# Spectral layers of a gated mixing kernel: z copied out of its bank by ScalarE, sum and low part made from the copies, one clamp moved to GpSimd

## The chip, the cores and the metric

The kernel runs on one core of one Trainium2 chip. A core has five engines, each with its own instruction queue that is worked off in order: TensorE (PE in the profile; PEld is its weight loading), VectorE (DVE), ScalarE (ACT), GpSimd (POOL) and SyncE (SP, which here only issues DMAs). The metric is the device time of one execution in microseconds (us). The kernel before takes 2457.5 us, the median of three runs (2455.3 to 2458.45).

## The reference

Two layers share an input and are mixed by a gate. Layer A is the spectral one: a real Fourier transform over 4096 tokens, a two-layer complex perceptron in four blocks of 160 channels on every frequency, a soft threshold, and the inverse transform. Layer B is a gated feed-forward network.

```python
x = A_x                                                  # A_x has shape (2, 1, 4096, 640)
g = _sigmoid((x * gate_w).sum(-1, keepdims=True))
a = _A_ref(x, A_w1, A_b1, A_w2, A_b2)
b = _B_ref(x, B_w_gate, B_w_up, B_w_down)
return g * a + (1 - g) * b

# _A_ref, per frequency; z has real part zr and imaginary part zi
hr = relu(zr @ w1[0] - zi @ w1[1] + b1[0]);  hi = relu(zi @ w1[0] + zr @ w1[1] + b1[1])
or_ = hr @ w2[0] - hi @ w2[1] + b2[0];       oi_ = hi @ w2[0] + hr @ w2[1] + b2[1]
# soft threshold at lam = 0.01, then irfft2
# _B_ref
(_gelu(x @ w_gate) * (x @ w_up)) @ w_down
```

## The kernel before

All matmuls of weight run on numbers that were split in two: a high part, which ScalarE makes by a copy that rounds (`high`, L292), and a low part, source minus high part, which VectorE makes (`low`, L295). A product is then three matmuls: high by high, high by low, low by high.

The program has four parts in time. Up to about 1316 us TensorE does the first two matrices of layer B, with the first stage of the Fourier transform (`a_step`) sprinkled in. From about 1316 to 1760 us come the spectral layers, which the change touches. Then follow the last matrix of layer B together with the second inverse stage, to the end. There is no planner: the order in which the Python code calls the engines is the order of each queue.

**The spectral layers** run as 64 steps, 4 for each of 16 chunks of 256 frequencies; the four steps of a chunk are its four channel blocks, n = 0 to 3. The chunk that is called wide (the second one, steps 4 to 7) has two more columns and a path of its own. One turn i of the loop issues, in this order:

- `main_z` for step i+1. Its core is `fwd2`: the second stage of the Fourier transform for 128 channels of a block, 4 matmuls at L1018 (8 in the trace, which shows each of these twice) into a PSUM bank `pz`, whose first half is the real part of z and whose second half the imaginary part, 256 columns each. Out of the bank come z high (L292), z low (L295), and the sum of both halves: ScalarE copies the second half to `zt` (L1029), VectorE adds the first half (L1030). The sum in turn is split into `zs` high and low, by a closure that `fwd2` returns and that is called later (`sums`). The sum lets three products stand for the four of a complex one.
- `mlp1` for step i: bank `pk` from zs (4 matmuls), copied out by ScalarE to `kc` (L1126); bank `pm` from z (8 matmuls); two adds on VectorE give `hs` (L1133); then `sums()` for step i+1; then relu and split into `h` (ScalarE L1089, VectorE L1090); bank `pl` for the 32 channels per block that do not fit in 128 (5 matmuls), taken out by ScalarE (L1139) and VectorE (L1140).
- `mlp2` for step i-1: two banks `py` of 16 matmuls each, taken out by ScalarE (`m`, L1170) and VectorE (`y`, L1171).
- `rest_of` for step i: relu of the 64 rows that L1140 wrote, to `hB` (L1143) and `hA` (L1144), both on ScalarE, and the low part from them on VectorE (L1145). hA and hB are used by `mlp2` of the next turn.
- In every odd turn, `inv1`: the first inverse stage, four banks `pi` of 3 matmuls each, taken out by ScalarE (L1206) and VectorE (L1208) in turn. In every even turn, `y_split`: y is split into `ys`, two tiles of 640 columns, both high parts on ScalarE, one low part on VectorE and one on GpSimd.
- Once a chunk, in the turn with i = 1 modulo 4 (below the rest turn), `rest`: the same `fwd2`, for the 4 x 32 remaining channels of the next chunk, issued ahead of `main_z`. Its z (named `zz`) and zs go through DRAM (`zld`) and come back four times as `zl` (`zl_load`, two turns ahead of their use). Its closure `end` runs at the end of the turn, ahead of `inv1`, and makes zs with the low part on GpSimd.

There are eight PSUM banks. They are handed out in turn, so a matmul that opens a bank waits for the last reader of what stood there eight hand-outs before. Two engines that read the same bank are ordered one behind the other too. An even turn takes 6 banks (pz, pk, pm, pl, py, py), an odd one 10, the one with `rest` 11. Thus pk takes the bank of the last pl when an odd turn came before it, and waits for the reader L1140; the third pi of an odd turn takes the bank of the same turn's main pz, the fourth that of its pk, and in the rest turn the second that of the rest's pz.

Of the kernel before, what the change touches and what calls it, by code (L numbers as in the profile page):

```python
# [10 lines left out]
F32 = mybir.dt.float32  # L11
F32R = mybir.dt.float32r
AF = mybir.ActivationFunctionType
OP = mybir.AluOpType

P = 128
# [6 lines left out]
CH = 256  # L23
CW = CH + 2
NCH = 8
# [211 lines left out]
def spectral_mix_kernel(ctx: ExitStack, tc: tile.TileContext, a):  # L237
    nc = tc.nc
    out = a["out"]

    def dr(t, off, ap):
        return bass.AP(tensor=t.tensor, offset=t.offset + off, ap=ap)
# [7 lines left out]
    def bank():  # L250
        return psum.tile([P, 512], F32, name="bank", tag="bank")
# [6 lines left out]
    def small(shape, dt=F32, name="small"):  # L258
        return pool.tile(shape, dt, name=name, tag="small", bufs=17)

    def tiny(shape, dt=F32, name="tiny"):
        return pool.tile(shape, dt, name=name, tag="tiny", bufs=15)
# [4 lines left out]
    def st(dst, src):  # L267
        late.append((dst, src))
# [22 lines left out]
    def high(dst, src, scale=1.0):  # L291
        nc.scalar.activation(dst, src, AF.Copy, scale=scale)  # L292

    def low(dst, src, hi, eng=nc.vector):
        eng.tensor_sub(dst, src, hi.bitcast(F32))  # L295

    def split(dst_h, dst_l, src, eng=nc.vector):

        high(dst_h, src)
        low(dst_l, src, dst_h, eng)  # L300

    def by_two(m):
        return m.rearrange("p (k i) -> p i k", k=2)
# [8 lines left out]
    def mms(dst, ops):  # L312
        for i, (l, r) in enumerate(ops):
            nc.tensor.matmul(dst, l, by_two(r), start=i == 0, stop=i == len(ops) - 1)  # L314
# [207 lines left out]
    def x_deep(gr, tp):  # L522


        o = {}
        F = XA[gr, tp] = {}

        def part(k):
# [3 lines left out]
            def tile():  # L532
# [5 lines left out]
                for j, n in enumerate(names):  # L538
                    F[n] = tuple(m[:, h, 320 * j:320 * j + 320] for h in range(2))
                return m  # L540
# [424 lines left out]
    chunks = [(0, 1), (0, 0)] + [(b, c) for b in range(2) for c in range(NCH) if (b, c) > (0, 1)]  # L965

    def zmid(b, c, shape, dt=F32, name="z"):
        return (big if wide(b, c) else mid)(shape, dt, name=name)

    def two(b, c, name):  # L970

        if wide(b, c):
            return [mid([P, 2, CW], F32R, name=name) for h in range(2)]
        t = mid([P, 2, 2, CH], F32R, name=name)
        return [t[:, h] for h in range(2)]
# [3 lines left out]
    def part_of(b, c, k):  # L979

        if not wide(b, c):
            return tiny([P, CH], name=("zt", "kc", "hs")[k])
        if not WT:
            WT.append(mid([P, 3, CW], name="wt"))
        return WT[0][:, k]
# [27 lines left out]
    def fwd2(b, c, o, z, zs=None):  # L1013

        pz = bank()
        for kp in range(4):
            ft = F2[0 if c == 0 and kp == 0 else 1]
            nc.tensor.matmul(pz.rearrange("p (r e k f) -> p k r e f", r=2, e=2, k=4)[:, kp], SC[b, c, kp][:, o:o + P],  # L1018
                             ft.rearrange("p (r e f) -> p r e f", r=2, e=2), start=True, stop=True)
        F = width(b, c)  # L1020
        if F > CH:
            zz = [z[h][:, :, :F].rearrange("p r (e n) -> p r e n", e=2)[..., :P] for h in range(2)]
            pr = pz.rearrange("p (r e n) -> p r e n", r=2, e=2)
        else:
            zz, pr = [z[h][:, :, :F] for h in range(2)], pz.rearrange("p (r n) -> p r n", r=2)
        if zs:
            t = part_of(b, c, 0)
            t4 = t[:, :F].rearrange("p (e n) -> p e n", e=2)[..., :P] if F > CH else t[:, :F]
            nc.scalar.activation(t4, pr[:, 1], AF.Copy)  # L1029
            nc.vector.tensor_add(t4, pr[:, 0], t4)  # L1030
        high(zz[0], pr)
        low(zz[1], pr, zz[0])
        if wide(b, c):
            pn = bank()
            for q in range(2):
                nc.tensor.matmul(pn[:, :4], SC[q, c, 0][:, o:o + P], fny[:, 4 * q:4 * q + 4], start=q == 0, stop=q == 1)
            split(*(z[h][:, :, :F].rearrange("p r (e n) -> p r e n", e=2)[..., P] for h in range(2)),
                  pn[:, :4].rearrange("p (r f) -> p r f", r=2))
            if zs:
                nc.vector.tensor_copy(t[:, :F].rearrange("p (e n) -> p e n", e=2)[..., P], pn[:, :2])  # L1040
        return lambda eng=nc.vector: split(zs[0][:, :F], zs[1][:, :F], t[:, :F], eng)
# [3 lines left out]
    def rest(b, c):  # L1045

        F = width(b, c)
        z = zmid(b, c, [P, 2, 2, F], F32R, name="zz")
        first = (b, c) == chunks[0]
        zs = small([P, 2, F], F32R, name="zs") if first else None  # L1050
        zs = [zs[:, h] if first else tiny([P, F], F32R, name="zs") for h in range(2)]
        sums = fwd2(b, c, 4 * P, [z[:, h] for h in range(2)], zs)
        d = zld[b][c]
        for h in range(2):
            st(dr(d, 3 * CW * h, [[6 * CW, P], [CW, 2], [1, F]]), z[:, h].bitcast(F32))

        def end():
            sums(nc.gpsimd)
            for h in range(2):
                st(dr(d, 3 * CW * h + 2 * CW, [[6 * CW, P], [1, F]]), zs[h].bitcast(F32))  # L1060
        later.append(end)

# [29 lines left out]
    def mlp1(b, c, n, sums):  # L1092
        F = width(b, c)
        z, (sh, sl) = Z.pop((b, c, n))
        w, wl = W1[n], W1L[n]
        t = ZL.pop((b, c, n))

        part = lambda k: (w[:, k:k + P], w[:, LOW1 + k:LOW1 + k + P])

        def group(dst, m):  # L1100
            r = 1 - m
            wh, wlo = part(OUT1[m])
            mms(dst, [(wh, z[0][:, r]), (wh, z[1][:, r]), (wlo, z[0][:, r]), (wl[:98, P + P * m:2 * P + P * m], t[:98, r])])

        def last(dst):

            for r in range(2):
                k = LAST1[r]
                nc.tensor.matmul(dst, w[:, k:k + P], by_two(z[0][:, r, :F]), start=r == 0, stop=False, skip_group_check=True)
                nc.tensor.matmul(dst, w[:, k:k + P], by_two(z[1][:, r, :F]), start=False, stop=False, skip_group_check=True)  # L1110
            nc.tensor.matmul(dst, wl[:, 384:], by_two(t[:, 3]), start=False, stop=True, skip_group_check=True)
        h = two(b, c, "h")
        if wide(b, c):
            if n < 2:
                x = small([P, 2, CW], F32R, name="hl")
                nc.gpsimd.memset(x[64:66, 1].bitcast(F32), 1.0)
                HW[n] = x[:, 0], x[:66, 1]
            hA, hB = HW[n % 2]
        else:
            hA, hB = hl1[n % 2], hl2[n % 2]  # L1120
        H[b, c, n] = (h, hA, hB)
        pk = bank()
        wh, wlo = part(OUT1["k"])
        mms(pk[:, :F], [(wh, sh[:, :F]), (wh, sl[:, :F]), (wlo, sh[:, :F]), (wl[:96, :P], t[:96, 2])])
        kc, hs = part_of(b, c, 1), (small if wide(b, c) else mid)([P, 2, F], name="hs")
        nc.scalar.activation(kc[:, :F], pk[:, :F], AF.Copy)  # L1126
        pm = [bank()] * 2 if F == CH else [bank(), bank()]
        for r in range(2):
            d = pm[r][:, r * CH:(r + 1) * CH] if F == CH else pm[r][:, :F]
            group(d, r)  # L1130
        for r in range(2):
            d = pm[r][:, r * CH:(r + 1) * CH] if F == CH else pm[r][:, :F]
            nc.vector.tensor_add(hs[:, r, :F], d, kc[:, :F])  # L1133
        sums()
        relu_split(h[0], h[1], hs)
        pl = bank()
        last(pl[:, :F])
        hs = part_of(b, c, 2)[:64]
        nc.scalar.activation(hs, pl[64:, :F], AF.Copy)  # L1139
        nc.vector.scalar_tensor_tensor(hs, pl[:64, :F], b1r[:, n:n + 1], hs, op0=OP.add, op1=OP.add)  # L1140

        def rest_of():
            nc.scalar.activation(hB[:64, :F], hs, AF.Relu)  # L1143
            nc.scalar.activation(hA[:64, :F], hs, AF.Relu)  # L1144
            nc.vector.scalar_tensor_tensor(hA[64:, :F], hs, 0.0, hB[:64, :F].bitcast(F32), op0=OP.max,  # L1145
                                           op1=OP.subtract)
        return rest_of
# [443 lines left out]
    for i, (gr, tp) in enumerate(keys):  # L1591
        if deep((gr, tp)) and tp % 2 == FIRST % 2:
            p, f = x_deep(gr, tp)
# [28 lines left out]
    for i, key in enumerate(keys):  # L1622
# [4 lines left out]
        if nxt:  # L1627
            if not i:
                x_raw(nxt)
            z = 7 * (nq - 1)  # L1630
# [13 lines left out]
        for j, t in enumerate(quads):  # L1644
# [10 lines left out]
            n = len(late)  # L1655
# [23 lines left out]
    for ch in range(1, 2 * NCH):  # L1679
        b, c = chunks[ch]  # L1680
# [27 lines left out]
    for i in range(S + 2):  # L1708
# [23 lines left out]
        if 0 <= i - 1 < S:  # L1732
            b, c, n = steps[i - 1]
# [10 lines left out]
    for i in range(len(c_seq)):  # L1744
        n = i + 1 if i + 1 < len(c_seq) else None
# [65 lines left out]
```

## Time and profile before

| | |
|---|---|
| median of 3 runs | 2457.5 us |
| the profiled execution, its own time | 2454.23 us |
| its span, first to last instruction | 2452.4 us |
| PE, PEld, DVE, ACT, POOL busy over the span | 99%, 97%, 81%, 60%, 7% |
| spectral layers | about 1316 to 1760 us |

How to read it: an engine's row gives start and duration of an instruction, and in brackets the idle time of the engine just before it with what ended it. Matmuls are pipelined: a matmul's duration is longer than the distance to the next one, so the distance between starts is what a matmul costs. The profiled execution is 3.3 us shorter than the median of the three runs.

### The profile page before, as it was taken

How to read it: one execution, taken by the hardware profiler on the slowest of the kernel's cores; microseconds unless marked ns; L12 is line 12 of the kernel's file. 1: busy time of each engine (PE TensorE's matmuls, PEld its weight loads, DVE VectorE, ACT ScalarE, POOL GpSimd, SP SyncE). 2: the span in 40 equal slices, each digit the busy share in tenths (PEclk: the TensorE clock that was granted, in tenths of full speed). 3: DMA queues.
4: the chain of work that ended last, by engine and by line, in shares of the span. 5: the costliest groups of instructions: out<-in, count | busy, mean ns of one | idle time of the engine just before them, and what ended most of it. 6: DMA issues, size and time to landing. Idle time of an engine off the chain costs nothing.

```text
span 2452.4 us, 50055 instructions
## 1 busy us (share of the span) xinstructions
PE 2415.7 (99%) x17983; PEld 2388.7 (97%) x17983; DVE 1980.7 (81%) x4175; ACT 1476.4 (60%) x3368; POOL 181.1 (7%) x286
## 2 busy tenths in 40 slices
PE   9999999999999999999999999999999999999999
PEld 9999999999999999999999888988899999999999
DVE  7777778777778888888758778787888988888887
ACT  5544456655556666666546777777755555555554
POOL 0111110000000000000001222212000000000000
PEclk9999999999999999999999999999999999999999
DMA  5665576777777768677765555667964455555443
GB/s 214 244 231 228 220 257 209 261 256 250 260 258 245 255 227 276 233 270 236 254 243 188 172 180 182 186 194 252 312 212 149 151 156 160 168 162 158 150 148 105
DMA packets 341315, 521.78 MB, mean 213 GB/s; under 512 B 28863, under 2 KB 217927, under 8 KB 341067
## 3 DMA queue, kind: packets, MB, share of 16 engines
q1 hardware_dynamic: 321002, 465.30, 57.1%
q0 software_dynamic: 20064, 53.29, 6.0%
q8 instruction: 142, 2.33, 0.4%
q14 instruction: 107, 0.87, 0.1%
HBM read 323.17 MB, written 195.30 MB: 211 GB/s over the span
## 4 chain that ended last, share of the span: by engine, by line
PE 81%; issue 6%; DMA 4%; DVE 4%; ACT 3%; SPq 1%; POOL 0%; ACTq 0%; DVEq 0%; POOLq 0%
PE bank L580 68%; PE bank L314 8%; PE bank L711 2%; PE bank L834 1%; DMA zl<-zl 1%; DVE hs L1133 1%; PE bank L1018 1%; DMA f<-in_f_dram 1%; ACT h L1089 1%; DMA wx<-wdf 1%; DMA scr<-is 1%; DVE zt L1030 1%; DMA xraw<-in_xT_dram 0%; DMA sc<-scr 0%; ACT kc L1126 0%
## 5 line engine op out<-in xcount | busy, mean ns | idle before, releaser
L580 PE MATMUL bank<-xo,w 128*128 128x320 f32 (+1 forms) x9000 | 1250.4, 297 | 0.7 <-ACT p L607 0.7
L580 PEld LDWEIGHTS bank<-xo,w 128*128 128x128 f32 x9000 | 1220.0, 189 | 2.0 <-ACT p L607 1.2
L580 PE MATMUL bank<-wx,ho 128*128 128x320 f32 x4608 | 632.5, 299 | 3.6 <-DMA wx<-wdf 2.4
L580 PEld LDWEIGHTS bank<-wx,ho 128*128 128x128 f32 x4608 | 627.8, 189 | 4.7 <-DMA wx<-wdf 2.9
L295 DVE TENSOR_TENSOR ho<-hraw,ho 128x640 fp32r<-128x640 f32 (+3 forms) x384 | 194.4, 541 | 25.4 <-ACT ho L292 23.4
L292 ACT ACTIVATE ho<-hraw 128x640 fp32r<-128x640 f32 x320 | 168.9, 571 | 37.6 <-PE bank L580 31.1
L607 ACT ACTIVATE u<-bank 128x320 f32<-128x320 f32 (+1 forms) x250 | 107.4, 430 | 135.9 <-PE bank L580 132.0
L657 DVE TENSOR_TENSOR u<-bank,u 128x320 f32<-128x320 f32 (+1 forms) x165 | 80.1, 485 | 81.9 <-ACT u L607 80.9
L295 DVE TENSOR_TENSOR xs<-xr,xs 64x640 fp32r<-64x640 f32 x128 | 105.0, 820 | 46.7 <-ACT xs L292 43.3
L836 DVE TENSOR_TENSOR as<-bank,as 64x320 f32<-64x320 f32 x256 | 113.9, 483 | 25.2 <-ACT as L835 23.4
L295 DVE TENSOR_TENSOR xo<-xraw,xo 128x640 fp32r<-128x640 f32 (+1 forms) x155 | 125.0, 807 | 8.7 <-ACT xo L292 6.8
L314 PE MATMUL bank<-wm,h 128*128 128x320 f32 (+1 forms) x792 | 129.4, 299 | 0.6 <-DVE zz L295 0.6
L607 ACT ACTIVATE p<-bank 128x320 f32<-128x320 f32 (+1 forms) x125 | 54.1, 432 | 118.7 <-PE bank L580 61.6
L835 ACT ACTIVATE as<-bank 64x320 f32<-64x320 f32 x256 | 96.6, 426 | 31.6 <-PE bank L834 28.4
L292 ACT ACTIVATE xo<-xraw 128x640 fp32r<-128x640 f32 (+1 forms) x155 | 111.7, 721 | 5.3 <-DMA xraw<-in_xT_dram 4.1
L314 PEld LDWEIGHTS bank<-wm,h 128*128 128x128 f32 (+1 forms) x792 | 111.7, 186 | 2.1 <-DVE zz L295 0.9
L1427 ACT ACTIVATE bank<-bank 128x320 f32<-128x320 f32 x31 | 13.1, 422 | 166.9 <-PE bank L580 166.9
L1421 DVE SCALAR_TENSOR_TENSOR uu<-bank,gs,uu 128x320 f32<-128x320 f32 x193 | 102.8, 547 | 11.4 <-PE bank L580 7.9
L1393 DVE SCALAR_TENSOR_TENSOR uu<-bank,gs,uu 128x320 f32<-128x320 f32 x120 | 57.8, 544 | 48.9 <-ACT uu L1392 48.9
L292 ACT ACTIVATE xs<-xr 64x640 fp32r<-64x640 f32 x128 | 93.4, 730 | 2.2 <-DMA hD<-h 0.4
L608 ACT ACTIVATE h<-bank 128x320 f32<-128x320 f32 (+1 forms) x165 | 71.1, 431 | 36.5 <-PE bank L580 33.1
L607 ACT ACTIVATE pb<-bank 128x320 f32<-128x320 f32 x80 | 34.9, 437 | 89.3 <-PE bank L580 89.3
(190 smaller groups left out, 3597.4 us busy)
## 6 DMA issues: line engine op xcount, KB each, us to landing
xo<-xD SPq DMA_DIRECT2D x96, 640.0 KB
xraw<-in_xT_dram SPq DMA_DIRECT2D x158, 320.0 KB
hD<-h SPq DMA_DIRECT2D x128, 320.0 KB
hraw<-hD SPq DMA_DIRECT2D x128, 320.0 KB
xD<-xo POOLq DMA_DIRECT2D x48, 640.0 KB, 4.4
sc<-scr SPq DMA_DIRECT2D x65, 320.0 KB
xr<-in_x_dram SPq DMA_DIRECT2D x64, 320.0 KB
scr<-as SPq DMA_DIRECT2D x64, 320.0 KB
```

The lines of the kernel that those rows point to most:

```text
L292: nc.scalar.activation(dst, src, AF.Copy, scale=scale)
L295: eng.tensor_sub(dst, src, hi.bitcast(F32))
L314: nc.tensor.matmul(dst, l, by_two(r), start=i == 0, stop=i == len(ops) - 1)
L580: nc.tensor.matmul(dst, l, by_two(r), start=first and i == 0, stop=i == len(ops) - 1, skip_group_check=True)
L607: copy = lambda d, s_: nc.scalar.activation(d, s_, AF.Copy)
L608: gelu = lambda d, s_: nc.scalar.activation(d, s_, AF.Gelu_apprx_tanh)
L657: nc.vector.tensor_add(u4, C, u4)
L711: nc.tensor.matmul(acc, l, by_two(r), start=first and i == 0, stop=i == 2, skip_group_check=True)
L835: nc.scalar.activation(stg[hi, cs], pa[lo, :320], AF.Copy)
L836: nc.vector.tensor_add(stg[hi, cs], pa[hi, :320], stg[hi, cs])
L1393: nc.vector.scalar_tensor_tensor(uu[n2][:, cs], po[:, :320], gs[b][:, k, n2:n2 + 1], uu[n2][:, cs], op0=OP.mult, op1=OP.add)
L1421: nc.vector.scalar_tensor_tensor(dst, x, g, dst, op0=OP.mult, op1=OP.add)
```

## The change

`fwd2` gets a second form, for chunks 0 and 2 to 11 (the wide one and the last four keep the first form). In it ScalarE copies both halves of z out of the bank, `zt` twice; VectorE adds the two copies in SBUF; and nothing else is done at once. The closure `end`, called where `sums` was called, makes z high from the bank (ScalarE), z low from the copies, one instruction per half (VectorE), and zs as before. In the first form, z high is now issued ahead of the add. In `rest`, the stores of zz move into `end`, behind the making of zz. In `rest_of`, hB is made by GpSimd instead of ScalarE.

```diff
@@ fwd2
         F = width(b, c)
+        if zs and F == CH and chunks.index((b, c)) < 2 * NCH - 4:
+            u = [tiny([P, CH], name="zt") for r in range(2)]
+            for r in range(2):
+                nc.scalar.activation(u[r], pz[:, CH * r:CH * r + CH], AF.Copy)
+            t = tiny([P, CH], name="zt")
+            nc.vector.tensor_add(t, u[0], u[1])
+
+            def end(eng=nc.vector):
+                high(z[0], pz.rearrange("p (r n) -> p r n", r=2))
+                for r in range(2):
+                    low(z[1][:, r], u[r], z[0][:, r])
+                split(zs[0][:, :F], zs[1][:, :F], t, eng)
+            return end
...
             nc.scalar.activation(t4, pr[:, 1], AF.Copy)
+        high(zz[0], pr)
+        if zs:
             nc.vector.tensor_add(t4, pr[:, 0], t4)
-        high(zz[0], pr)
         low(zz[1], pr, zz[0])
@@ rest
         d = zld[b][c]
-        for h in range(2):
-            st(dr(d, 3 * CW * h, [[6 * CW, P], [CW, 2], [1, F]]), z[:, h].bitcast(F32))
 
         def end():
             sums(nc.gpsimd)
             for h in range(2):
+                st(dr(d, 3 * CW * h, [[6 * CW, P], [CW, 2], [1, F]]), z[:, h].bitcast(F32))
                 st(dr(d, 3 * CW * h + 2 * CW, [[6 * CW, P], [1, F]]), zs[h].bitcast(F32))
@@ mlp1, rest_of
-            nc.scalar.activation(hB[:64, :F], hs, AF.Relu)
+            nc.gpsimd.tensor_scalar(hB[:64, :F], hs, 0.0, None, op0=OP.max)
             nc.scalar.activation(hA[:64, :F], hs, AF.Relu)
```

Counted over the program, ScalarE gets 55 copies of 128x256 more (zt) and 64 clamps fewer (hB); on VectorE 55 z low of 512 columns become 110 of 256 and 55 adds change their operands from bank and tile to two tiles; GpSimd gets 64 clamps. TensorE's work is the same. Behind the inserted lines, line numbers of the changed kernel are 13 higher.

How the queues change, at three places.

ScalarE in a turn of the second form without `rest`, from the copies out of pz to the relus of the 64 rows (hl is hA and hB; "waits" names the engines whose results an instruction waits for). Before:

```order
L1029 ACTIVATE zt<-bank 128x256 [waits PE_49]
L292 ACTIVATE z<-bank 128x512 [waits DVE_49]
L1126 ACTIVATE kc<-bank 128x256 [waits PE_49,Activation_49]
L292 ACTIVATE zs<-zt 128x256
L1089 ACTIVATE h<-hs 128x512 [waits DVE_49]
L1139 ACTIVATE hs<-bank 64x256 [waits PE_49,Activation_49]
L1170 ACTIVATE m<-bank,neg2lam 128x320 [waits PE_49,Activation_49] x2
L1143 ACTIVATE hl_17102<-hs 64x256 [waits DVE_49]
L1144 ACTIVATE hl_17101<-hs 64x256
```

And in the changed kernel:

```order
L1024 ACTIVATE zt<-bank 128x256 [waits PE_49,Activation_49]
L1024 ACTIVATE zt<-bank 128x256
L1139 ACTIVATE kc<-bank 128x256 [waits PE_49,Activation_49]
L292 ACTIVATE z<-bank 128x512
L292 ACTIVATE zs<-zt 128x256 [waits DVE_49]
L1102 ACTIVATE h<-hs 128x512 [waits DVE_49]
L1152 ACTIVATE hs<-bank 64x256 [waits DMAHW1_49,PE_49]
L1183 ACTIVATE m<-bank,neg2lam 128x320 [waits PE_49,Activation_49] x2
L1157 ACTIVATE hl_17110<-hs 64x256 [waits DVE_49]
```

z high moved from ahead of kc to behind it, and its wait for VectorE is gone; kc stands behind two copies that wait for TensorE only.

VectorE in the same part of a turn. Before:

```order
L1030 TENSOR_TENSOR zt<-bank,zt 128x256 [waits Activation_49]
L295 TENSOR_TENSOR z<-bank,z 128x512 [waits Activation_49]
L1133 TENSOR_TENSOR hs<-bank,kc 128x256 [waits PE_49,Activation_49]
L1133 TENSOR_TENSOR hs<-bank,kc 128x256
L295 TENSOR_TENSOR zs<-zt,zs 128x256 [waits DVE_49,Activation_49]
L1090 SCALAR_TENSOR_TENSOR h<-hs,h 128x512 [waits Activation_49]
L1140 SCALAR_TENSOR_TENSOR hs<-bank,b1r,hs 64x256 [waits Activation_49]
L1171 SCALAR_TENSOR_TENSOR y<-bank,m 128x8x40 [waits Activation_49] x2
L1145 SCALAR_TENSOR_TENSOR hl_17101<-hs,hl_17102 64x256 [waits Activation_49]
```

And in the changed kernel, to the low part of the 64 rows:

```order
L1026 TENSOR_TENSOR zt<-zt 128x256 [waits Activation_49]
L1146 TENSOR_TENSOR hs<-bank,kc 128x256 [waits PE_49,Activation_49]
L1146 TENSOR_TENSOR hs<-bank,kc 128x256
L295 TENSOR_TENSOR z<-zt,z 128x256 [waits Activation_49]
L295 TENSOR_TENSOR z<-zt,z 128x256
L295 TENSOR_TENSOR zs<-zt,zs 128x256 [waits Activation_49]
L1103 SCALAR_TENSOR_TENSOR h<-hs,h 128x512 [waits Activation_49]
L1153 SCALAR_TENSOR_TENSOR hs<-bank,b1r,hs 64x256 [waits DMAHW1_49,Activation_49]
L1184 SCALAR_TENSOR_TENSOR y<-bank,m 128x8x40 [waits DMAHW4_49,Activation_49]
L1184 SCALAR_TENSOR_TENSOR y<-bank,m 128x8x40 [waits DMAHW5_49,Activation_49]
L1158 SCALAR_TENSOR_TENSOR hl_17110<-hs,hl_17111 64x256 [waits Pool_49]
```

z low moved from ahead of the hs adds to behind them and is two instructions; the last one, the low part of hA, now waits for GpSimd.

ScalarE at the end of the turn with `rest`, from the bank readers of `mlp2` to those of `inv1`, in the changed kernel (before, zz was issued at the start of the turn, right behind its zt):

```order
L1183 ACTIVATE m<-bank,neg2lam 128x320 [waits PE_49,Activation_49] x2
L1157 ACTIVATE hl_17110<-hs 64x256 [waits DVE_49]
L292 ACTIVATE zz<-bank 128x512
L292 ACTIVATE zs<-zt 128x256
L1219 ACTIVATE is<-bank 128x320 [waits PE_49] x2
```

and TensorE there, the first two pi (ys by the table i), before:

```order
L314 MATMUL bank<-ys,i_17095 128x320 [waits Activation_49]
L314 MATMUL bank<-ys,i_17095 128x320
L314 MATMUL bank<-ys,i_17095 128x320 [waits DVE_49]
L314 MATMUL bank<-ny,xn 128x320 [waits Pool_49]
L314 MATMUL bank<-ny,xn 128x320
L314 MATMUL bank<-ys,i_17095 128x320 [waits DVE_49]
L314 MATMUL bank<-ys,i_17095 128x320 x4
```

and in the changed kernel:

```order
L314 MATMUL bank<-ys,i_17100 128x320 [waits Activation_49]
L314 MATMUL bank<-ys,i_17100 128x320
L314 MATMUL bank<-ys,i_17100 128x320 [waits DVE_49]
L314 MATMUL bank<-ny,xn 128x320 [waits Pool_49]
L314 MATMUL bank<-ny,xn 128x320
L314 MATMUL bank<-ys,i_17100 128x320 [waits Activation_49]
L314 MATMUL bank<-ys,i_17100 128x320 x4
```

The second pi takes the bank of the rest's pz. Its wait moved from VectorE (zz low, early in the turn) to ScalarE (zz high, now at the turn's end).

## The prediction

> **What bounds the kernel now.** I read the stretches of the spectral part first: windows, with length, busy time of PE, PEld, DVE, ACT and POOL, granted clock, DMA share and GB/s. The second row is the ten chunks that get the second form, the third holds the first three of the last four chunks, the fourth the way into the next part.
>
> ```profile
> 1316.00:1372.00 56.00, 53.61 (x423) 50.61 (x422) 43.94 (x106) 41.57 (x105) 11.54 (x16) 1.00 0.56 178
> 1372.00:1650.00 278.00, 260.75 (x1983) 245.94 (x1981) 220.90 (x484) 210.95 (x513) 58.46 (x70) 1.00 0.60 183
> 1650.00:1730.00 80.00, 74.74 (x571) 70.97 (x572) 63.98 (x140) 60.72 (x149) 15.93 (x19) 1.00 0.78 246
> 1730.00:1790.00 60.00, 53.62 (x387) 50.60 (x386) 48.69 (x101) 38.98 (x93) 3.69 (x7) 1.00 1.02 342
> ```
>
> The clock is full throughout and no engine is: weight loading rests 32.1 of 278 us, DVE 57.1, ACT 67. In the fourth row the DMA engines are full instead. So who waits in the second row? The waits there, in us in total, times, longest:
>
> ```profile
> PEld bank L314 <- DVE hs L1140: 15.3, 19, 0.8
> PEld bank L314 <- ACT kc L1126: 9.4, 19, 0.9
> PEld bank L1018 <- DVE hs L1133: 3.2, 19, 0.2
> PEld bank L314 <- DVE zz L295: 1.9, 9, 0.5
> DVE z L295 <- ACT z L292: 26.8, 40, 0.7
> DVE h L1090 <- ACT h L1089: 14.7, 40, 0.4
> DVE zz L295 <- ACT zz L292: 6.0, 9, 0.7
> ACT z L292 <- DVE zt L1030: 26.3, 40, 0.9
> ```
>
> TensorE's four waits (29.8 us) are all for a bank that a reader frees late. DVE's three waits are for ACT; with them DVE is taken for 268 of 278 us. That is a relay: ACT and DVE hand z, hs and h to and fro, and TensorE hangs on them by its eight banks. The timeline of one turn shows the relay, ACT first and then DVE.
>
> ```profile
> 1561.52 1.35 ACT L292 ACTIVATE ys<-y 128x640 fp32r<-128x640 f32 x2
> 1562.77 0.36 ACT L1029 ACTIVATE zt<-bank 128x256 f32<-128x256 f32 x1
> 1563.62 0.60 ACT L292 ACTIVATE z<-bank 128x512 fp32r<-128x512 f32 x1 [0.49 <-DVE zt L1030]
> 1564.12 0.38 ACT L1126 ACTIVATE kc<-bank 128x256 f32<-128x256 f32 x1
> 1564.38 0.42 ACT L292 ACTIVATE zs<-zt 128x256 fp32r<-128x256 f32 x1
> 1565.64 0.63 ACT L1089 ACTIVATE h<-hs 128x512 fp32r<-128x512 f32 x1 [0.84 <-DVE hs L1133]
> 1566.30 0.38 ACT L1139 ACTIVATE hs<-bank 64x256 f32<-64x256 f32 x1
> 1566.70 0.94 ACT L1170 ACTIVATE m<-bank,neg2lam 128x320 f32<-128x320 f32 x2
> 1567.54 0.41 ACT L1143 ACTIVATE hl<-hs 64x256 fp32r<-64x256 f32 x1
> ```
>
> ```profile
> 1563.16 0.42 DVE L1030 TENSOR_TENSOR zt<-bank,zt 128x256 f32<-128x256 f32 x1
> 1564.25 0.69 DVE L295 TENSOR_TENSOR z<-bank,z 128x512 fp32r<-128x512 f32 x1 [0.66 <-ACT z L292]
> 1564.86 0.74 DVE L1133 TENSOR_TENSOR hs<-bank,kc 128x256 f32<-128x256 f32 x2
> 1565.52 0.42 DVE L295 TENSOR_TENSOR zs<-zt,zs 128x256 fp32r<-128x256 f32 x1
> 1566.31 0.69 DVE L1090 SCALAR_TENSOR_TENSOR h<-hs,h 128x512 fp32r<-128x512 f32 x1 [0.37 <-ACT h L1089]
> 1566.91 0.47 DVE L1140 SCALAR_TENSOR_TENSOR hs<-bank,b1r,hs 64x256 f32<-64x256 f32 x1
> 1567.31 0.92 DVE L1171 SCALAR_TENSOR_TENSOR y<-bank,m 128x320 f32<-128x320 f32 x2
> 1568.26 0.42 DVE L1145 SCALAR_TENSOR_TENSOR hl<-hs,hl 64x256 fp32r<-64x256 f32 x1
> ```
>
> ACT copies zt, idles until DVE has added, copies z; only then comes kc, which TensorE waits for, and DVE idles 0.66 until z is there. What would TensorE take without the waits? Its own timeline, starts and durations:
>
> ```profile
> 1554.46 0.60 PE L314 MATMUL bank<-zs,wm 128*128 128x256 f32 x3 [0.62 <-DVE hs L1140]
> ...
> 1567.44 0.60 PE L314 MATMUL bank<-zs,wm 128*128 128x256 f32 x3 [0.56 <-DVE hs L1140]
> ...
> 1571.62 1.95 PE L1018 MATMUL bank<-f,sc 128*128 128x128 f32 x16
> 1573.33 0.58 PE L314 MATMUL bank<-zs,wm 128*128 128x256 f32 x3
> ...
> 1577.48 0.57 PE L314 MATMUL bank<-ys,i 128*128 128x320 f32 x3
> 1577.89 0.43 PE L314 MATMUL bank<-ny,xn 128*128 128x320 f32 x2
> ...
> 1582.10 0.60 PE L314 MATMUL bank<-zs,wm 128*128 128x256 f32 x3 [0.62 <-DVE hs L1140]
> ```
>
> By distances of starts: pk to the last py 1571.62 - 1567.44 = 4.18; a pz half of 1573.33 - 1571.62, 0.86; a pi, from the first ys row to the ny row behind it, 0.41. A chunk (four turns from pk to the last py, five pz with the rest's, eight pi) without waits is 4 x 4.18 + 5 x 0.86 + 8 x 0.41 = 24.3 us. It takes 1582.10 - 1554.46 = 27.64. So 3.3 us a chunk are there to be had, and no more.
>
> **The change part by part.** Engine time first. ACT gains 55 x 0.36 and loses 64 x 0.41: 6 us less. On DVE a z low of 0.69 becomes two of 0.42, at most 55 x 0.15 = 8 us more; the add from two tiles I price like zs, also 0.42 from two tiles, so as now. A chunk's DVE work is then 22.1 + 0.8 = 22.9 of 24.3 us: covered by TensorE, with 1.4 to spare; without that cover it would cost its 8 us. GpSimd's clamp is not in the trace. Its bounds are the nearest rows there, a memset and the 640-column subtraction:
>
> ```profile
> 1575.98 1.55 POOL L295 TENSOR_TENSOR ys<-y,ys 128x640 fp32r<-128x640 f32 x1 [10.39 <-ACT ys L292]
> 1577.59 0.52 POOL L1066 MEMSET zl<- 2x512 f32 x1
> 1583.35 0.73 POOL L295 TENSOR_TENSOR zs<-zt,zs 128x256 fp32r<-128x256 f32 x1 [5.25 <-issue]
> ```
>
> I take 0.73, the same 256 columns. Only DVE's low part of hA waits for it, behind two y of 0.92 together that start when the clamp does; 0.73 is hidden there, 1.55 would hold DVE, and with it ys or the next zt, by 0.6 us. SP's stores of zz leave later, but they always stood ahead of the zs stores in the same queue, which already waited for the turn's end; the loads behind gain no wait.
>
> Now the waits, by re-timing two turns with TensorE running free, zero at its pz. I let ACT read 0.2 behind the last matmul of a bank (estimate: a matmul's row is about 0.17 longer than its distance, and h above starts 0.04 after hs ends).
>
> *Even turn.* TensorE: pz to 0.86, pk 1.36, pm 2.25, pl 2.81, py 3.92 and 5.04. ACT: both zt 1.06 to 1.75, kc to 2.06, z to 2.54, nothing of it waiting for DVE. DVE: hs 2.45 to 3.20, z, z and zs to 4.25. ACT h to 3.87; DVE h to 4.9, L1153 done at 5.3. The pk that may need it starts at 6.76: 1.5 us spare. ACT m waits for the second py (to 5.76), hA 6.07, ys to 7.3; POOL ys 7.35 to 8.9.
>
> *Rest turn.* TensorE: two pz to 6.76, pk 7.26, pm 8.15, pl 8.71, py 9.82 and 10.94, first pi to 11.35. ACT comes from ys: four zt 7.28 to 8.59, kc to 8.9, z, zs 9.7; DVE hs 9.05 to 9.8; ACT h 10.46; DVE z, z, zs, h to 11.5, L1153 11.9; ACT hs and both m to 11.7, hA from 11.92, and only behind it zz, 12.23 to 12.83. The second pi sits in that bank: it starts at 12.87 instead of 11.35, **1.5 us late**. This is the change's new wait. Behind it the queues are level again: the next turn's zt waits for its own pz. In the other two turns the same chain gives L1153 at 5.3 after the turn's pz while the pk that wants the bank comes at 7.5 (a turn with four pi), and z high at 2.5 after it while the pi that wants its bank comes at 5.9. No release is late there.
>
> A chunk is then 24.3 + 1.5 = 25.8: 1.84 less, **18.4 us** for ten (bounds: 0, and 33 with no wait left). The last chunks keep the first form in the new order: zt, z and kc follow each other on ACT, DVE's add waits for z high (same bank) and z low follows at once, so one hand-over between the engines is left of three; L1140 comes some 0.2 later in the re-timing than L1153 does above (5.5 against 5.3), and the rest's bank is freed at the start of the turn, so there is no new stall; of the 9.0 us that weight loading rests in the third row I take **6** (0 to 9), since the DMA engines are busy 0.78 there. In the first row weight loading rests 5.4, with chunk 0 in the second form and the wide one in the first; I take **2** (0 to 5), less than half, since the loop only fills there. The fourth is bound by DMA: **0**. Sum 26.4. From the profiled execution's 2454.2 that is 2427.8; the median of the runs was 3.3 higher, so **2431 us** is what I put against it.
>
> **A row and a rule.** While POOL made ys from 1575.98 to 1577.53, DVE's add ran undisturbed:
>
> ```profile
> 1576.14 0.43 DVE L1030 TENSOR_TENSOR zt<-bank,zt 128x256 f32<-128x256 f32 x1
> ```
>
> That add has one operand in a bank; the new one has both in SBUF. The Trainium skill (SBUF — State Buffer, section "Who interferes with whom") says that a VectorE instruction with two SBUF inputs and a GpSimd instruction that reads SBUF exclude each other, the later one being blocked to the earlier one's end. No run here shows it.
>
> **The rivals.**
> 1. *DVE's add queues behind POOL's ys.* For it: POOL's ys ends at 8.9 in the re-timing, the rest turn's first add is due at 7.97. Against: the row above, which is another kind of add. If it waits, add, add and hs end 0.65 later, zz too: stall 2.15, a chunk gains 1.2, the sum is 12 + 8 = 20, **2438 us**. (It is the mechanism of the rule just named.)
> 2. *The relay only changes its shape.* From hs to L1140 is 1566.91 - 1564.86 = 2.05 now; with both z low in between it is some 2.3. What the earlier kc wins (0.5 for the wait of z, 0.5 for z itself) must outlast this 0.25 and the second zt (0.31). For it: DVE is the fuller of the two, and with its present waits it has no time left. Against: the waits that go are DVE's own, 0.66 of them ahead of z. If ACT's lead is used up all the same, TensorE keeps its 3.3: **2455 us**.
> 3. *Slower: the clamp on GpSimd.* DVE's low part of hA waits for it; ys, adds, hs and L1153 stand behind; zz, and so the second pi, come later by its length less 0.9 (the y) and 0.5 (DVE's idle time ahead of the rest turn). The chunk loses from 1.4 + 1.84 = 3.2 us of clamp on; at 4.5 the ten chunks lose 13 and the other terms go: **2470 us**. Against: 0.73 for a two-operand instruction.
> 4. *No stall in the rest turn either*, if ACT runs ahead there: 33 + 8 = 41, **2416 us**. That needs zz 1.5 us earlier, for which hA would have to leave ACT's queue ahead of it. Against: hA must wait for L1153 at 11.9, and zz stands behind hA.
>
> **How the numbers follow.** Forecast 0.46, rivals 0.25, 0.13, 0.06, 0.10. A change under 0.2% (5 us) can't be told from none. Faster: forecast, rivals 1 and 4 and a quarter of 2, 0.84; same 0.09; slower 0.07. The range, 2417 to 2453, leaves out half of rival 4, much of 2 and all of 3.
>
> **What would show it.** Right: ACT z and kc no longer wait for DVE; waits for L1140 (now L1153) and kc nearly gone from TensorE; in their place one wait a chunk of about 1.5 us, for ACT's zz; chunk distance 25.8. Wrong: that distance at 27 or more, a clamp over 1.5 us, DVE's adds of zt longer than 0.43, or new waits for the loads of sc and zl.

## The result and the profile after

The changed kernel takes 2425.95 us (median of 4 runs, 2423.75 to 2428.02), the kernel before 2457.97 in the same comparison (2455.30 to 2459.84): ratio 0.987, 95% interval 0.9853 to 0.9888. The profiled execution takes 2423.75 us with a span of 2422.0, against 2454.23 and 2452.4 before, so 30.4 us of span are to be found. The prediction had put 26.4 there, and 2431 us against the median.

The windows of the changed kernel, the same four stretches and the same columns as in the prediction:

```profile
1316.00:1372.00 56.00, 55.99 (x456) 54.35 (x455) 50.51 (x123) 43.70 (x112) 18.58 (x24) 1.00 0.60 187
1372.00:1650.00 278.00, 270.81 (x2169) 266.69 (x2168) 261.58 (x578) 236.74 (x567) 105.50 (x122) 1.00 0.66 202
1650.00:1730.00 80.00, 75.82 (x578) 74.61 (x577) 65.62 (x144) 58.28 (x137) 24.37 (x29) 0.96 0.93 298
1730.00:1790.00 60.00, 56.34 (x397) 55.26 (x397) 50.93 (x104) 33.66 (x77) 1.10 (x2) 0.97 0.80 275
```

In the second row weight loading rests 11.3 us of 278 where it rested 32.1, and VectorE went from 220.90 to 261.58: it is now the fullest engine beside TensorE. In the third and fourth rows the granted clock is below 1, which it was nowhere before.

Where the time was won is read from the starts of the pz of a rest turn (16 matmuls of line 1018 together, or their first part), from TensorE's timeline, first in the kernel before and then in the changed one. The first two marks of each bound the ten chunks:

```profile
1377.28 1.95 PE L1018 MATMUL bank<-f,sc 128*128 128x128 f32 x16
...
1654.70 1.95 PE L1018 MATMUL bank<-f,sc 128*128 128x128 f32 x16
...
1682.38 0.91 PE L1018 MATMUL bank<-f,sc 128*128 128x128 f32 x4
```

```profile
1373.95 1.95 PE L1018 MATMUL bank<-f,sc 128*128 128x128 f32 x16
...
1628.13 1.95 PE L1018 MATMUL bank<-f,sc 128*128 128x128 f32 x16
...
1652.43 0.46 PE L1018 MATMUL bank<-f,sc 128*128 128x128 f32 x2
1654.42 0.49 PE L1018 MATMUL bank<-f,sc 128*128 128x128 f32 x2 [1.54 <-DMA sc<-scr]
```

Up to the first mark 3.3 us are won; over the ten chunks 277.42 became 254.18, 23.2 us; over the next chunk, the first in the first form with the new order, 27.68 became 24.30, 3.4 us. Together 29.95 of the 30.4: behind that mark next to nothing is won. The chunk distance is 25.4 us against 27.7 before and 25.8 forecast; the late one takes just the 24.3 that the prediction had worked out as the floor.

The waits of TensorE's weight loads in the second stretch, and two of ScalarE's there (us in total, times, longest):

```profile
ACT zs L292 <- DVE zt L1026: 20.2, 33, 0.9
...
ACT h L1102 <- DVE hs L1146: 13.6, 42, 0.8
...
PEld bank L1018 <- DMA sc<-scr: 4.2, 7, 1.2
...
PEld bank L314 <- DVE hs L1153: 3.5, 6, 0.6
PEld bank L1018 <- DVE hs L1153: 2.9, 4, 1.1
```

29.8 us of waits became 10.6. No wait for ScalarE is left among TensorE's, and the wait of 1.5 us for zz that the forecast put into each chunk is not there. ScalarE's z and kc wait for nobody; it waits for VectorE only behind them, at zs. And VectorE's new adds are late. A rest turn, and adds of later turns, from the timeline (start, length, engine and line; in brackets the idle time before it and who ended it):

```profile
1529.74 1.18 ACT L1024 ACTIVATE zt<-bank 128x256 f32<-128x256 f32 x4
...
1529.97 1.71 POOL L295 TENSOR_TENSOR ys<-y,ys 128x640 fp32r<-128x640 f32 x1 [1.01 <-DMA zl<-zl]
...
1530.41 1.89 DVE L1026 TENSOR_TENSOR zt<-zt 128x256 f32<-128x256 f32 x2
...
1530.80 0.40 ACT L1139 ACTIVATE kc<-bank 128x256 f32<-128x256 f32 x1
...
1531.06 0.63 ACT L292 ACTIVATE z<-bank 128x512 fp32r<-128x512 f32 x1
...
1532.34 0.42 ACT L292 ACTIVATE zs<-zt 128x256 fp32r<-128x256 f32 x1 [0.65 <-DVE zt L1026]
...
1532.84 1.79 PE L314 MATMUL bank<-ys,i 128*128 128x320 f32 x12
...
1535.02 1.16 PE L1018 MATMUL bank<-f,sc 128*128 128x128 f32 x8 [0.38 <-DVE hs L1153]
...
1535.32 0.57 ACT L292 ACTIVATE zz<-bank 128x512 fp32r<-128x512 f32 x1
...
1536.35 0.73 POOL L295 TENSOR_TENSOR zs<-zt,zs 128x256 fp32r<-128x256 f32 x1 [0.46 <-ACT zs L292]
1536.38 0.98 DVE L295 TENSOR_TENSOR zz<-zt,zz 128x256 fp32r<-128x256 f32 x1
...
1543.47 1.67 POOL L295 TENSOR_TENSOR ys<-y,ys 128x640 fp32r<-128x640 f32 x1 [1.04 <-ACT ys L292]
...
1543.90 1.53 DVE L1026 TENSOR_TENSOR zt<-zt 128x256 f32<-128x256 f32 x1 [0.16 <-ACT zt L1024]
...
1550.31 0.41 DVE L1026 TENSOR_TENSOR zt<-zt 128x256 f32<-128x256 f32 x1
```

An add of zt takes 0.41 us when GpSimd is idle (1550.31) and 1.53 when it starts inside GpSimd's ys (1543.90): it ends 0.29 us behind ys, at 1545.43 against 1545.14. zz's low part does the same behind zs (1537.36 against 1537.08). The groups of the second stretch, of VectorE and then of GpSimd (count | busy, mean ns):

```profile
L1026 DVE TENSOR_TENSOR zt<-zt 128x256 f32<-128x256 f32 x47 | 37.5, 812 | 3.1 <-ACT zt L1024 1.9
...
L295 DVE TENSOR_TENSOR zz<-zt,zz 128x256 fp32r<-128x256 f32 x18 | 11.9, 697 | 0.3
...
L1045 DVE TENSOR_TENSOR zt<-bank,zt 128x256 f32<-128x256 f32 x8 | 3.4, 421 | 1.6 <-ACT z L292 0.9 <-ACT zz L292 0.7
```

```profile
L1156 POOL TENSOR_SCALAR hl<-hs 64x256 fp32r<-64x256 f32 x44 | 37.0, 840 | 142.8 <-DVE hs L1153 127.6 <-DMA scr<-is 15.2
L295 POOL TENSOR_TENSOR ys<-y,ys 128x640 fp32r<-128x640 f32 x22 | 36.8, 1672 | 24.5 <-ACT ys L292 15.9 <-DMA zl<-zl 8.6
```

The adds from two copies take 812 ns on average, those that still read a bank 421. Of the 47, 18 start inside GpSimd's ys. GpSimd's ys grew from 1.55 to 1.67; the clamp takes 0.84.

### The profile page after: what moved, and what is told of

The parts are those of the page before. It is cut to its first block, busy times and chain, and to the rows that moved or that the text cites. A ratio compares the mean times of both kernels' runs of the same rounds, so it can differ in the third digit from the quotient of the medians.

```text
span 2422.0 us, 50047 instructions
## 1 busy us (share of the span) xinstructions
PE 2399.7 (99%) x17983; PEld 2389.4 (99%) x17983; DVE 2001.5 (83%) x4230; ACT 1477.8 (61%) x3359; POOL 239.9 (10%) x350
## 4 chain that ended last, share of the span: by engine, by line
PE 84%; issue 6%; DMA 5%; DVE 3%; ACT 1%; POOL 0%; SPq 0%; POOLq 0%; ACTq 0%; DVEq 0%
PE bank L580 69%; PE bank L314 9%; PE bank L711 2%; PE bank L1018 2%; PE bank L834 1%; DMA sc<-scr 1%; DMA f<-in_f_dram 1%; DMA scr<-is 1%; DMA zl<-zl 1%; DMA xraw<-in_xT_dram 0%; DVE hs L1146 0%; ACT ys L292 0%; DMA wx<-wdf 0%; DVE z L295 0%; DMA s<-scr 0%
## 5 line engine op out<-in xcount | busy, mean ns | idle before, releaser
L1018 PE MATMUL bank<-f,sc 128*128 128x128 f32 x640 | 87.1, 281 | 6.9 <-DMA sc<-scr 4.7
```

## The experiments

**Theory P**, formed from this trace: the gain comes from the order (z's high part on ScalarE no longer waits for VectorE's add); the copies by themselves cost something, because a VectorE instruction with both inputs in SBUF stands still while GpSimd reads SBUF. **The rivals**: the copies carry the gain by freeing the bank early; or the clamp's move does, by unloading ScalarE; or VectorE is simply full and the hold does not matter. All edits are against the changed kernel, each was timed beside the kernel before (2456.3 in the first comparison, 2456.6 in the others).

**No copies.** All chunks take the first form, with the new order and the clamp on GpSimd.

```diff
-        if zs and F == CH and chunks.index((b, c)) < 2 * NCH - 4:
+        if False:
```

> All chunks in the first form with z high ahead of the add; clamp on GpSimd; no copies. Theory P (the copies' adds and low parts, with both operands in SBUF, are held up by GpSimd's ys; only the order of z high frees the relay): a chunk takes TensorE's 24.3 us instead of the changed kernel's 25.3, ten chunks 10 us, so about 2416 us against 2426, adds at 0.42. Theory C (it is the copies that free the relay, since nobody waits on the bank): part of the old waits comes back, 26 to 27 us a chunk, 2433 to 2443.

2417.72 us, ratio 0.984 (0.9825 to 0.9855): 8 us below the changed kernel. Its windows and weight-load waits, second stretch:

```profile
1372.00:1650.00 278.00, 273.66 (x2191) 270.55 (x2190) 241.73 (x540) 221.49 (x529) 111.07 (x125) 0.99 0.69 211
```

```profile
PEld bank L314 <- DVE hs L1153: 1.1, 3, 0.8
```

VectorE is busy 241.73 in place of 261.58 while TensorE does more in the same time, and the waits for VectorE fell from 6.4 to 1.1. GpSimd's ys still takes 1.68 here, but the adds, one of whose inputs is a bank, take 0.42 each. So the copies are not needed for the gain. In the company of the other two parts they cost 8 us.

**The clamp back on ScalarE.**

```diff
-            nc.gpsimd.tensor_scalar(hB[:64, :F], hs, 0.0, None, op0=OP.max)
+            nc.scalar.activation(hB[:64, :F], hs, AF.Relu)
```

> The changed kernel with the clamp back on ScalarE. Theory P: GpSimd is left with ys, zs and memsets; the adds behind ys stay held up, so 25.3 us a chunk or little less (0.3 for the low part of hA that no longer waits), 2423 to 2426. Rival (ScalarE needs the 0.41 a turn that it was relieved of): kc and z late by 0.4 a turn, 1.6 a chunk, 2440.

2426.76 us, ratio 0.9881 (0.9865 to 0.9898): no different from the changed kernel. With the copies in place the clamp's engine does not matter.

**The old order in the first form**, so in the chunks that have no copies.

```diff
-        high(zz[0], pr)
         if zs:
             nc.vector.tensor_add(t4, pr[:, 0], t4)
+        high(zz[0], pr)
```

> The changed kernel, but where the first form is kept (wide chunk and last four) the add stands ahead of z high again. If those chunks' 24.3 us come from the order alone, the chunk ahead of the DMA-filled end goes back to 27.6 and the wide one too: 2431 to 2434. If the order there brings nothing because the DMA sets the end anyway: 2426.

2432.50 us, ratio 0.99 (0.9885 to 0.9915): 6.5 us are lost, as expected. The chunk behind the ten takes 26.8 here and 24.3 in the changed kernel, which is 2.5 of it. The other 4 lie ahead of the ten: the first mark stands at 1378.0 here, at 1373.95 in the changed kernel and at 1377.28 in the kernel before. In the wide chunk TensorE waits 1.85 us here for ScalarE's line 1139, a wait that the new order does not have. Without that order nothing is left of what was won ahead of the ten chunks.

**Both ys lows on VectorE**, which takes away what holds the adds, at 0.82 us of VectorE every second turn.

```diff
-                  nc.gpsimd if j == 1 and (b, c, pb) < (1, NCH - 2, 1) else nc.vector)
+                  nc.vector)
```

> The changed kernel with both low parts of ys on VectorE (0.82 more for VectorE in every even turn, 1.64 a chunk), so GpSimd reads SBUF only for the clamp and for zs of the rest. Theory P: the adds fall from up to 1.57 to 0.42, 2.2 us a chunk, which more than pays: 24.7 to 25.2 us a chunk, 2420 to 2425. Rival (the adds are long for another reason and VectorE is simply the bound): 27 us a chunk, 2442.

2420.85 us, ratio 0.9855 (0.984 to 0.9869). The adds, in the same stretch:

```profile
L1026 DVE TENSOR_TENSOR zt<-zt 128x256 f32<-128x256 f32 x47 | 19.1, 417 | 3.1 <-ACT zt L1024 2.8
...
L295 DVE TENSOR_TENSOR zz<-zt,zz 128x256 fp32r<-128x256 f32 x18 | 11.4, 675 | 0.3
```

Work was added to the fullest engine and the kernel did not become slower: the adds went from 37.5 to 19.1 us, and the median is 5.1 us below that of the changed kernel. zz, beside GpSimd's zs, which stayed, is held as before. That rules out that VectorE is simply full.

**The add from the bank.** The copies stay, and only one input of the add is changed.

```diff
-            nc.vector.tensor_add(t, u[0], u[1])
+            nc.vector.tensor_add(t, pz[:, :CH], u[1])
```

> The changed kernel in which the add of zt reads its first half from the bank and its second half from ScalarE's copy; both copies are still made, and the low parts are still made from them, so that ScalarE and VectorE have the same number of instructions. Theory P (a VectorE add with both inputs in SBUF stands still while GpSimd reads two inputs from SBUF): the adds of zt take 0.42 to 0.45 us each with no maximum above 0.6, GpSimd's ys keeps 1.55 to 1.60 us, and the time is 2420 (2417 to 2423); the low parts of z, which also read two copies, can still be held, so it need not reach the 2417.7 of the kernel without copies. Rival (the time is lost because the copies take ScalarE and VectorE more work, or because the add waits for two ScalarE instructions): 2426 as the changed kernel.

2421.63 us, ratio 0.986 (0.9846 to 0.9875). The adds and TensorE's remaining wait for VectorE, in the same stretch:

```profile
L1026 DVE TENSOR_TENSOR zt<-bank,zt 128x256 f32<-128x256 f32 x47 | 19.8, 421 | 8.9 <-ACT zt L1024 7.7
```

```profile
PEld bank L1018 <- DVE hs L1153: 1.2, 1, 1.2
```

The number of instructions on each engine and their shapes are those of the changed kernel; the place of one input decides how long the adds take, and TensorE's waits for VectorE fall from 6.4 to 1.2 us, next to the 1.1 of the kernel without copies. What that is worth in time is less sure. The medians are 4.3 and 5.1 us lower, but they are of four runs each, from different comparisons: the changed kernel took 2423.75 to 2428.02, this one 2419.19 to 2425.78, the one with ys on VectorE 2418.45 to 2423.66, and the intervals of their ratios overlap. In the traces the ten chunks take 251.0 us with either edit, 254.2 in the changed kernel and 247.5 without copies. One chunk of this kernel takes 28.35 where the next takes 24.5; in it TensorE waits 1.89 us for sc and then runs 3.4 us at half clock. So it is not shown that the copies cost anything beside the hold: the rest of the 8 us may be this wait, and it stays open.

**Each part alone.** Three kernels complete the table: the order alone (first form everywhere, clamp on ScalarE), the copies alone (the clamp on ScalarE, the old order in the chunks without copies), and the clamp alone (first form in the old order). The later issue of two stores is in all of them. The copies bring a new order with them, since z high in their chunks waits for no add; no kernel here has the copies with the old order in the same chunks.

```diff
order alone and clamp alone:
-        if zs and F == CH and chunks.index((b, c)) < 2 * NCH - 4:
+        if False:
copies alone and clamp alone:
-        high(zz[0], pr)
...
+        high(zz[0], pr)
order alone and copies alone:
-            nc.gpsimd.tensor_scalar(hB[:64, :F], hs, 0.0, None, op0=OP.max)
+            nc.scalar.activation(hB[:64, :F], hs, AF.Relu)
```

> The kernel before with the order of the step alone changed (the high part of z ahead of the add; with it the later issue of the two stores); no copies of both halves, and the clamp for hl stays on ScalarE. Theory P: the order carries the whole gain, so 2418 (2415 to 2421), as the kernel with order and clamp on GpSimd (2417.7). Rival (the move of the clamp frees ScalarE, which the chunk needs): 2425 to 2435.

> The kernel before with the copies of both halves alone (and the later issue of the two stores); in the chunks without copies the old order, add ahead of the high part; the clamp for hl on ScalarE. In the chunks with copies the order is changed all the same, since the add no longer reads the bank. Theory P: 2432 (2429 to 2436), as the changed kernel with the old order in its other chunks (2432.5), the clamp being worth nothing. Rival: over 2440, if ScalarE, which now has one copy more and the clamp, becomes what each chunk waits for.

> The kernel before with the clamp for hl alone on GpSimd (and the later issue of the two stores). The relay from ScalarE to VectorE and back on the bank of z stays as it was. Theory P: 2452 to 2460, no difference that can be told, since ScalarE waits in each chunk for VectorE and not for itself. Rival: 2435 to 2448, if ScalarE's own work holds the relay up.

Measured: order alone 2429.68, ratio 0.9892 (0.9876 to 0.9909); copies alone 2432.47 with a wide spread (2428.25 to 2441.55), 0.9908 (0.9884 to 0.9932); clamp alone 2453.06, 0.9984 (0.9975 to 0.9993). All eight combinations, medians in us, from four comparisons in which the kernel before took 2456.3 to 2458.0:

| | clamp on ScalarE | clamp on GpSimd |
|---|---|---|
| no copies, old order | 2456.6 (before) | 2453.1 |
| no copies, new order | 2429.7 | **2417.7** |
| copies, old order elsewhere | 2432.5 | 2432.5 |
| copies, new order elsewhere | 2426.8 | 2426.0 (the change) |

The profiled executions show where the time goes (us; the waits are those of weight loading from 1372 to 1650, for banks that ScalarE or VectorE reads, and for the loads of sc):

| kernel | ten chunks | waits for readers | waits for sc |
|---|---|---|---|
| before | 277.4 | 29.8 | 0 |
| clamp alone | 274.1 | 25.8 | 0 |
| order alone | 255.7 | 8.9 | 3.2 |
| copies alone | 260.0 | 4.2 | 10.9 |
| the change, clamp on ScalarE | 253.4 | 2.9 | 6.9 |
| the change | 254.2 | 6.4 | 4.2 |
| order and clamp, no copies | 247.5 | 1.1 | 5.0 |

Where the waits for readers shrink, TensorE comes to wait for the loads of sc. The copies alone were profiled in their slowest execution, the 2441.55; there these loads are most of TensorE's waits.

The order alone brings 27 us. It ends at 2429.7 and not at theory P's 2418, and the rival of that run was right: once the order is changed, the clamp's move brings 12 us, though it is worth 3.5 without the new order and nothing with the copies. TensorE's largest wait with the order alone, second stretch, and a place where it arises:

```profile
PEld bank L314 <- DVE hs L1153: 8.9, 15, 0.8
```

```profile
1442.24 0.41 ACT L1156 ACTIVATE hl<-hs 64x256 fp32r<-64x256 f32 x1
1442.54 0.41 ACT L1157 ACTIVATE hl<-hs 64x256 fp32r<-64x256 f32 x1
...
1442.86 1.35 ACT L292 ACTIVATE ys<-y 128x640 fp32r<-128x640 f32 x2
...
1444.37 0.58 ACT L292 ACTIVATE z<-bank 128x512 fp32r<-128x512 f32 x1
...
1444.99 0.42 DVE L1045 TENSOR_TENSOR zt<-bank,zt 128x256 f32<-128x256 f32 x1 [0.55 <-ACT z L292]
...
1447.98 0.47 DVE L1153 SCALAR_TENSOR_TENSOR hs<-bank,b1r,hs 64x256 f32<-64x256 f32 x1
...
1448.50 0.60 PE L314 MATMUL bank<-zs,wm 128*128 128x256 f32 x3 [0.59 <-DVE hs L1153]
```

Without the copies the add must wait for z's high part, which reads the same bank; that stands behind ys on ScalarE, and ys behind the clamp. From the clamp to hs of line 1153 there is no slack, and TensorE waits 0.59 at its end. Taking the clamp out of ScalarE's queue shortens that line by 0.3 us a turn (1442.24 to 1442.54); in the kernel without copies the wait of 8.9 us is down to 1.1. In the copies form ScalarE waits 20.2 us for VectorE at zs, so a shorter queue on ScalarE should gain nothing, and nothing was gained. With the clamp on ScalarE the waits for readers are even smaller and those for sc larger (2.9 and 6.9 against 6.4 and 4.2), so the equal times are a balance, which no run here takes apart.

**The best kernel with both ys lows on VectorE**, the same edit that took 5 us off the median above.

> The kernel without copies (2417.7, order and clamp changed) with both ys lows on VectorE. With the copies this step gained 5 us (2426.0 to 2420.9). Theory P (GpSimd's two-input reads hurt only VectorE instructions with both inputs in SBUF, which are few here: the adds of zt read a bank): nothing is gained, 2416 to 2421, VectorE having 0.82 us more to do every second turn. Rival (GpSimd's ys slows VectorE or the transfers in general): 2413 or less.

2429.31 us, ratio 0.9888 (0.9873 to 0.9903): it costs 11.6 us. The rival, that GpSimd's ys is harmful as such, is refuted; theory P, which expected no change, missed this cost. TensorE's largest wait, and a place where it arises:

```profile
PEld bank L314 <- DVE hs L1153: 10.8, 18, 0.8
```

```profile
1441.77 1.56 DVE L295 TENSOR_TENSOR ys<-y,ys 128x640 fp32r<-128x640 f32 x2
...
1443.24 0.42 DVE L1045 TENSOR_TENSOR zt<-bank,zt 128x256 f32<-128x256 f32 x1
...
1443.70 0.42 ACT L292 ACTIVATE zs<-zt 128x256 fp32r<-128x256 f32 x1 [0.47 <-DVE zt L1045]
...
1446.75 0.60 PE L314 MATMUL bank<-zs,wm 128*128 128x256 f32 x3 [0.62 <-DVE hs L1153]
```

It is the same line as with the clamp, entered on VectorE: ys ahead of the add delays zs, hs, h, and the bank that TensorE wants.

**The best kernel with the loads of sc issued one turn earlier.**

```diff
-            at(4 * ch - 4 - lead[0], 0, sc_load, b, c)
+            at(4 * ch - 5 - lead[0], 0, sc_load, b, c)
```

> The kernel without copies (2417.7) with the loads of sc issued one turn earlier. In its trace TensorE still waits for sc (in all 3.2 us from 1372 to 1600, 1.7 us more around 1645), and the half clock of 3.4 us follows that wait. If the loads come late because they are issued late: these waits and the half clock after them go, 2411 to 2414. Rival (they come late because the queue in front of them is long, or because their buffers come free late): 2416 to 2422, or slower where an earlier place in the queue holds up loads of zl.

2417.81 us, ratio 0.9846 (0.9829 to 0.9862): nothing is gained. TensorE's waits from 1600 to 1800, first without and then with the earlier loads:

```profile
PE bank L314 <- DMA zl<-zl: 3.9, 2, 2.3
...
PE bank L1018 <- DMA sc<-scr: 1.7, 3, 0.8
```

```profile
PE bank L314 <- DMA zl<-zl: 8.2, 4, 3.5
```

The waits for sc went, there and in the ten chunks (246.4 us against 247.5), and the profiled execution, 2415.79 us, has no half clock in it; but the waits for zl grew by 4.3 us. In the stretch where the DMA engines are full the earlier place in the queue moved the wait to another load.

## Why the prediction was right

- **The bound.** Right in its cause: TensorE hung on the relay between ScalarE and VectorE through its banks. The floor of 24.3 us a chunk was a little high: one late chunk took just that and the kernel without copies (and with the clamp on GpSimd) takes 24.75, but chunks of 24.03 us occur where the adds read a bank and where both ys lows are on VectorE.
- **What the parts are worth.** The prediction gave the ten chunks' gain to the copies and let the new order work only in the last chunks. The table puts it elsewhere: the order alone gives 27 us, the copies alone, with the order that they bring, about as much (24, in a wide spread), and the order with the clamp's move 39. The diff had suggested the copies as the main part, and the prediction never re-timed the ten chunks in the first form with the new order.
- **The ten chunks, 18.4 us forecast, 23.2 measured, and for another reason.** The step that failed is the stall of 1.5 us at the second pi, "the second pi sits in that bank". In the trace the pi matmuls run unbroken from 1532.84 to 1534.6, while ScalarE reads zz at 1535.32, later even than the 1534.2 of the re-timing. So that pi is in another bank. The program as built numbers the banks: in such a turn of the kernel before, the rest's pz has bank 0 and the four pi have 2, 0, 1 and 7; of the changed kernel, the rest's pz has 4 and the pi have 2, 1, 0 and 5. Banks are not "handed out in turn", as was said of the kernel before, but in the order in which their last readers are issued. (In the kernel before, too, the third pi has the bank of pk and the fourth that of the main pz, not the reverse.) zz high is now issued at the turn's end, behind the last readers of the other banks, so the rest's bank goes out last and becomes the next turn's pl. The second pi has the bank of pk, and the ScalarE instruction that it waits for is the early kc, not zz. The pz of the next turn has the bank of pl and waits for line 1153 instead, 0.38 us.
- **What stands in its place** is rival 1, VectorE's adds behind GpSimd's ys, which the forecast put at nothing. Its mechanism was right, and there were more holds than the one of 0.65 us a chunk that was priced. The rows show the adds at 812 ns against 421, 0.39 us more each for more than four a chunk, and zz at 697 besides. Part of it is absorbed: TensorE's waits for VectorE are 6.4 us in all, and the two edits that take the hold off the adds leave 1.2 and 2.6 of them and shorten the ten chunks by 3.2 us. Two errors of opposite sign, a stall of 15 us that was not there and a hold that was left out, brought the forecast within 5 us of the result. That is luck; the mechanism of the ten chunks was forecast wrong.
- **VectorE at 22.9 of 24.3 us a chunk** was right for the work itself: in the kernel whose adds read the bank it is busy 227.5 us in its ten chunks, 22.7 a chunk, and in the changed kernel 240.3. The hold took 1.3 of the 1.4 us to spare.
- **The clamp.** Estimated 0.73 by its columns, measured 0.84, inside its bounds. It was priced as a cost that hides; that taking it off ScalarE could be worth 12 us without the copies was not seen.
- **First and last chunks.** 2 forecast, 3.3 measured, which is lost with the new order in the wide chunk; 6 forecast, 3.4 + 0.5 measured. The first of the last chunks gained what the floor allows; behind it the loads of sc came late (1.54 us at 1654.42), in a row whose DMA engines are busy 0.93. 0 for the last stretch was right.
- **Among the signs named as wrong**, two came: adds longer than 0.43, and new waits for sc, 4.2 us in the ten chunks.

## What to carry to other kernels

Before a relay between two engines is broken by copying its data, try the order of the two instructions that read the shared bank: here swapping them, with one instruction moved off the engine that then led, was worth 39 us and needed no copy. An instruction is worth moving only if it stands in the line that ends at the awaited release; the clamp's move gained 12, 3.5 or 0 us, and ys on VectorE cost 11.6 without the copies and nothing with them, as that line changed, so parts of a change must be timed in combination. When an input of a VectorE instruction is moved from a bank to SBUF, look at what GpSimd reads at that time.

## What the runs showed of the hardware

**VectorE and GpSimd exclude each other for two SBUF inputs.** The add of 128x256 takes 0.42 us with one input in a bank, also while GpSimd's ys runs, and up to 1.57 with both in SBUF; it ends 0.28 to 0.29 us behind GpSimd's instruction. It works the other way round too: in the kernel without copies GpSimd's zs starts 0.37 to 0.39 us before the end of VectorE's low part of hA, whose inputs both lie in SBUF, and takes 0.96 to 0.99 us; in the kernel before, where no such instruction ran at its start, it took 0.73. The hold counts as busy time in the row of the instruction that is held. The Trainium skill (SBUF — State Buffer, "Who interferes with whom") states this exclusion; all three arrangements tried here agree with it.

**The clock falls to half for 3.41 us after a half-idle stretch.** The changed kernel, windows of 3.41 us around its stall for sc, columns as above (busy PE second, granted clock third from the end):

```profile
1651.43:1654.84 3.41, 1.77 (x11) 1.25 (x9) 2.85 (x8) 3.21 (x7) 0.84 (x1) 1.00 0.95 299
1654.84:1658.25 3.41, 2.98 (x13) 2.61 (x13) 1.03 (x2) 1.17 (x3) 2.18 (x2) 0.50 1.01 337
1658.25:1661.67 3.42, 3.42 (x18) 3.42 (x18) 2.09 (x6) 1.67 (x4) 0.00 (x0) 0.50 0.98 378
```

TensorE rests 1.6 of 3.41 us and then two whole windows run at half clock. The stretches at half clock in the runs here last 3.41 or 6.83 us, and TensorE was busy at most 2.1 us in the window ahead of each. A low window does not always bring one: at 1658.15 the order alone had 2.06 busy and kept its clock. The Trainium skill (TensorE: Matmul & The Clock Gate, "What's actually happening") gives a free-running window of 3413 ns, which agrees; by the rule in its section "HAM oscillation — how this bites in real kernels" (no idle gaps of TensorE over some 3.4 us) nothing should have fallen here, where the longest single gap was 1.5 us, and the trace decides. What it costs is not shown apart from the wait ahead of it. The profiled execution with the earlier loads of sc ran at full clock throughout and took 2415.79 us, the one without them 2417.36; the other three runs with the earlier loads had a mean clock of 0.998 to 0.999 and took up to 2420.97.
